# Ordering the first and last 128 columns so that their 64 KB stores have 32, not 4, steps in the outer dimension

## Chip, cores and metric

One core of a Trainium2 chip. The metric is the device time of one execution in microseconds, the median over several executions, all fast, that is, none is over 1.5% above the fastest of its kernel. The span in the profile is some 1.8 us shorter than that time. Where two kernels are compared by runs, they ran on the same chip in the same rounds; where that is not so, the text says it.

## The reference

A polynomial-sketch linear attention (4 batches, 4 heads, 1088 tokens, head size 32), whose output becomes `x` of 4352 rows by 128, is followed by a mixture of 4 experts that are all computed for all rows:

```python
x = attn_out.transpose(0, 2, 1, 3).reshape(B * S, H * D)      # 4352 x 128
p = domain_probs / (domain_probs.sum(-1, keepdims=True) + 1e-09)
for e in range(4):
    h = np.maximum(x @ w1[e], 0.0)                            # 128 -> 1024
    out += p[:, e:e + 1] * (h @ w2[e])                        # 1024 -> 128
```

## The kernel before

The attention leaves `x` transposed in `xT`, 128 features by 4352 columns. A batch has 34 tokens for each of 32 groups; column `32*c + j` of a batch is token `34*j + c`. The columns are worked off in 11 chunks. Nine of them go through a Strassen-like scheme; the first and the last, of 128 columns, are "plain": their second product has the 128 tokens on the partitions, so that the result can be stored as it is, without a transpose. With 128 columns a plain chunk holds four token offsets of each of the 32 groups, and partition `32*a + j` is token `34*j + c + a`.

```python
def keep_warm(n):                      # products on zeros: TensorE busy before its data are there
    for _ in range(n):
        wp = psum(ps_h, "h")
        nc.tensor.matmul(wp[:, :], warm[:, 0:P], warm[:, :], start=True, stop=True)
keep_warm(11)
...
for i, t in enumerate((0, (B - 1) * S + G - 4)):          # gate rows of the two plain chunks
    nc.sync.dma_start(
        ends[:, i, :], bass.AP(domain_probs.tensor, domain_probs.offset + t * E, [[E, 4], [G * E, 32], [1, E]]))
...
nc.vector.tensor_tensor(                                  # last product of the attention
    out=xT[:, S * b + c : S * b + c + n], in0=nd[1][:, 0:n], in1=rb[:, 0:n], op=ALU.mult)
...
if e == E - 1:                                            # plain chunk: all four experts added up
    t = (START[m] // S) * S + START[m] % S // 32
    nc.sync.dma_start(
        bass.AP(out.tensor, out.offset + t * DM, [[DM, 4], [G * DM, 32], [1, DM]]), total.pop(m)[:, :])
```

The last of these stores is the last thing that the kernel does. The kernel is divided below into three parts that add up to the span: the *start*, up to the first expert matmul (`h<-xT,w_sb`); the *body*, from there to the issue of the last store; and the *end*, from that issue to the last instruction.

Of the kernel before, what the change touches and what calls it, by code (L numbers as in the profile page):

```python
# [11 lines left out]
ALU = mybir.AluOpType  # L12
# [4 lines left out]
def _ap(t, p0: int, np_: int, off: int, free):  # L17

    p = list(t.ap)[0]
    return bass.AP(t.tensor, t.offset + p0 * p[0] + off, [[p[0], np_]] + [list(d) for d in free])  # L20
# [3 lines left out]
def kernel(  # L24
# [23 lines left out]
    nc = tc.nc  # L48

    P = 128  # L50
    HP = 64
    B, H, S, D = q.shape
    E, DM, F = w1.shape
    R = 8
    R2 = 2 * R
    G = S // 32
# [26 lines left out]
    def psum(pool, tag):  # L83
        return pool.tile([P, 512], F32, tag=tag, name=tag)
# [59 lines left out]
    ends = cpool.tile([P, 2, E], F32, name="ends")  # L144
    e_sum = cpool.tile([P, 2, 3], F32, name="e_sum")
    for i, t in enumerate((0, (B - 1) * S + G - 4)):
        nc.sync.dma_start(
            ends[:, i, :], bass.AP(domain_probs.tensor, domain_probs.offset + t * E, [[E, 4], [G * E, 32], [1, E]])
        )
    load_rows(q, 0, "qn", slice(P, S))  # L150
    for e in range(E):
# [20 lines left out]
    def keep_warm(n):  # L172

        for _ in range(n):
            wp = psum(ps_h, "h")
            nc.tensor.matmul(wp[:, :], warm[:, 0:P], warm[:, :], start=True, stop=True)  # L176

    keep_warm(11)


    turn = [0]
# [2 lines left out]
    def on_side(out, weights, moving, **flags):  # L184

        s = turn[0]
        turn[0] = 1 - s
        nc.tensor.matmul(out(s), weights(s), moving(s), **flags)  # L188
# [114 lines left out]
    xT = cpool.tile([P, B * S], F32, name="xT")  # L303
# [115 lines left out]
    def attend(b, c, n, qp):  # L419


        nd = [psum(ps_n, "den"), psum(ps_n, "num")]
        for i in range(2):
            for _ in range(2):
                on_side(
                    lambda s: nd[i][half[s], 0:n],
                    lambda s: kvzs[b][:, s, 1 - i, :],
                    lambda s: qp[s][:, 0:n],
                    start=True,
                    stop=True,  # L430
                )
        yield
        dT = apool.tile([P, QW], F32, tag="dT", name="dT")
        nc.vector.transpose(dT[:, 0:n], nd[0][:, 0:n])
        yield
        rc = apool.tile([P, QW // 32], F32, tag="rc", name="rc")
        nc.vector.tensor_scalar(
            out=rc[:, 0 : n // 32], in0=_ap(dT, 0, P, 0, [[32, n // 32]]), scalar1=1e-6, scalar2=1.0, op0=ALU.add, op1=ALU.mult
        )
        nc.vector.reciprocal(rc[:, 0 : n // 32], rc[:, 0 : n // 32])  # L440
        rb = apool.tile([P, QW], F32, tag="rb", name="rb")
        nc.vector.transpose(
            _ap(rb, 0, P, 0, [[32, n // 32], [1, 32]]), _ap(rc, 0, P, 0, [[1, n // 32], [0, 32]])
        )
        yield
        nc.vector.tensor_tensor(
            out=xT[:, S * b + c : S * b + c + n], in0=nd[1][:, 0:n], in1=rb[:, 0:n], op=ALU.mult
        )
        have[0] += n
        yield  # L450

    def queries(b, c, n):
        qT = query_turn(b, c, n)
        yield
        yield
        yield
        qc = psum(ps_f, "f")
        both(qc[:, 0:n], sq[:, :], qT[:, 0:n], start=True, stop=True)
        yield
        qf = apool.tile([P, QW], F32, tag="qf", name="qf")  # L460
        nc.vector.stream_shuffle(in_=qc[:, 0:n], out=qf[:, 0:n], mask=mask_lo)
        yield
        nc.vector.tensor_tensor(out=qf[:, 0:n], in0=qc[:, 0:n], in1=qf[:, 0:n], op=ALU.add)
        yield
        qb = apool.tile([P, QW], F32, tag="qb", name="qb")
        nc.vector.stream_shuffle(in_=qf[:, 0:n], out=qb[:, 0:n], mask=mask_b)
        yield
        qp = query_tiles()
        for x in range(2):
            qa = apool.tile([P, QW], F32, tag="qa", name="qa")  # L470
            nc.vector.stream_shuffle(in_=qf[:, 0:n], out=qa[:, 0:n], mask=mask_a[x])
            yield
            for p in range(2):
                query_product(qp, p, x, n, qa, qb)
                yield
        yield
        yield
        yield from attend(b, c, n, qp)
# [18 lines left out]
    def start():  # L497
# [36 lines left out]
        for x in range(2):  # L534
            for p in range(2):
                query_product(qp, p, x, n, fq[1 + x], qb)
        key_divide(b, kv)
        first = attend(b, 0, n, qp)
        next(first)
        keep_warm(4)  # L540
# [20 lines left out]
    hid, acc, total = {}, {}, {}  # L561
    NP = FB // 2

    def plain(m):
        return m in (0, NC - 1)
# [57 lines left out]
    def second(i):  # L623
        m, kq = steps[i]
        n, (e, f) = CHUNKS[m], divmod(kq, NP)
        hd = hid.pop(i)
        if plain(m):

            if f == 0:
                acc[m] = psum(ps_o, f"o{e % 2}")  # L630
            for j in range(2):
                for _ in range(2):
                    on_side(
                        lambda s: acc[m][half[s], 0:DM],
                        lambda s: hd[:, n * j + HP * s : n * j + HP * s + HP],
                        lambda s: w2_sb[:, e, 2 * f + j, :],
                        start=(f == j == 0),
                        stop=(f == NP - 1 and j == 1),
                    )
            if f == NP - 1:  # L640
                p_e = ends[:, 1 if m else 0, e : e + 1]
                if e == 0:
                    total[m] = mpool.tile([P, P], F32, tag="end", name="end")
                    nc.vector.tensor_scalar(
                        out=total[m][:, :], in0=acc[m][:, 0:DM], scalar1=p_e, scalar2=None, op0=ALU.mult
                    )
                else:
                    nc.vector.scalar_tensor_tensor(  # L648
                        out=total[m][:, :], in0=acc[m][:, 0:DM], scalar=p_e, in1=total[m][:, :], op0=ALU.mult, op1=ALU.add
                    )  # L650
                if e == E - 1:
                    t = (START[m] // S) * S + START[m] % S // 32
                    nc.sync.dma_start(
                        bass.AP(out.tensor, out.offset + t * DM, [[DM, 4], [G * DM, 32], [1, DM]]), total.pop(m)[:, :]
                    )
            return
        if f == 0:
            acc[m, e] = [psum(ps_o, "o0"), psum(ps_o, "o1")]
            begun[:] = [0, 0]
        w = n // 2  # L660
        blk = lambda a, j: w2_sb[:, e, 2 * f + j, HP * a : HP * a + HP]
        new = lambda a: w2s[:, e, f, a, :]
        place = lambda a: hd[:, w * a : w * a + w]

        todo = (
            [(blk(0, 0), place(0)), (new(3), place(3)), (blk(0, 1), place(2)), (new(1), place(6))],
            [(new(2), place(5)), (new(0), place(4)), (blk(1, 1), place(7)), (new(1), place(6))],
        )
        at = [0, 0]
        for _ in range(7):  # L670
            s = turn[0]
            p = at[s]
            at[s] += 1

            fresh = p >= begun[s]
            begun[s] = max(begun[s], p + 1)
            wt, mv = todo[s][p]
            on_side(
                lambda s: acc[m, e][p // 2][half[s], w * (p % 2) : w * (p % 2) + w],
                lambda s: wt,  # L680
                lambda s: mv,
                start=(fresh and p % 2 == 0),
                stop=(f == NP - 1),
                skip_group_check=True,
            )
# [81 lines left out]
    for i in range(len(steps) + LA):  # L767
        if i < len(steps):
            m, kq = steps[i]
# [29 lines left out]
        if i >= LA:  # L799
            second(i - LA)  # L800
            mm, kk = steps[i - LA]
            if kk % NP == NP - 1 and not plain(mm):
                ending = chain(ending, gather(mm, kk // NP))
            else:
                next(ending, None)
# [29 lines left out]
```

## Time and profile before

| | before |
|---|---|
| time, median of 4 runs | 496.27 us (496.11 to 496.53) |
| profiled run: time, span | 495.9, 494.1 us |
| start: first expert matmul at | 14.10 us |
| body: 14.10 to 490.55 | 476.45 us, PE busy 476.04 |
| end: 490.55 to 494.12 | 3.57 us |
| last store: issue, first packet after issue, data | 0.60, 1.23, 0.92 us |

"First packet" and "data" (from the first packet's start to the last one's end) come from the trace's records of single DMA packets.

### The profile page before, as it was taken

Reading aid. Unit: us, or ns where it says so; the run is one execution under the profiler, and the core shown is the slowest. Engines: PE = TensorE matmul, PEld = TensorE weight load, DVE = VectorE, ACT = ScalarE, POOL = GpSimd, SP = SyncE. Lnnn points to the kernel's source line nnn. Section 1 sums busy time; section 2 is a strip of 40 time slices with the busy share of each in tenths; the row PEclk is TensorE's granted clock in tenths of the full one; section 3 lists DMA queues with packets and bytes.
Section 4 is the critical chain, followed back from the end, with each engine's and each line's share of the span. In section 5 each row is a group of like instructions: output and inputs, shape, how many; then the busy total and the mean of one; then the engine's idle time right before and its main releaser. Section 6 shows DMA issues by size and latency. Waiting matters only on the chain.

```text
span 494.1 us, 11020 instructions
## 1 busy us (share of the span) xinstructions
PE 487.7 (99%) x4435; PEld 373.7 (76%) x4435; DVE 323.2 (65%) x751; ACT 244.2 (49%) x487; POOL 227.2 (46%) x260
## 2 busy tenths in 40 slices
PE   8999999999999999999999999999999999999996
PEld 5887877777777777777777777777777777778996
DVE  6759666777677576758566647468656657765642
ACT  3344464545454634545445554445445445566751
POOL 6051464435445354425455445335455446555570
PEclk9999999999999999999999999999999999999999
DMA  7981030021002320021002100021001100110000
GB/s 215 277 294 54 2 90 3 1 87 21 0 2 87 85 73 0 1 87 23 0 2 86 21 1 1 2 86 22 2 1 54 22 1 1 44 23 2 15 3 17
DMA packets 29618, 22.36 MB, mean 45 GB/s; under 512 B 19968, under 2 KB 26752, under 8 KB 29184
## 3 DMA queue, kind: packets, MB, share of 16 engines
q1 hardware_dynamic: 29552, 21.66, 15.2%
q8 instruction: 35, 0.57, 0.5%
q14 instruction: 15, 0.12, 0.1%
q10 hardware_dynamic: 16, 0.00, 0.0%
HBM read 19.35 MB, written 2.31 MB: 44 GB/s over the span
## 4 chain that ended last, share of the span: by engine, by line
PE 98%; DVE 1%; DMA 0%; POOL 0%; issue 0%; DVEq 0%
PE h L188 50%; PE o L188 40%; PE f L188 4%; PE den L188 2%; PE num L188 2%; DMA s_raw<-in_S_dram 0%; PE h L176 0%; POOL sr L241 0%; POOL sp L236 0%; DVE end L648 0%; DVE s_e L200 0%; DVE kvz L374 0%; DVE s_f L200 0%; DVE s_T L228 0%; DVE s_hl L227 0%
## 5 line engine op out<-in xcount | busy, mean ns | idle before, releaser
L584 DVE SCALAR_TENSOR_TENSOR hid<-h,hid 128x256 f32<-128x256 f32 (+6 forms) x432 | 203.7, 472 | 146.9 <-ACT hid L609 138.7
L188 PE MATMUL h<-xT,w_sb 128*64 128x512 f32 (+4 forms) x1408 | 298.3, 495 | 0.4 <-PE h L176 0.4
L609 ACT ACTIVATE hid<-h 128x512 f32<-128x512 f32 (+3 forms) x288 | 158.3, 550 | 200.3 <-PE h L188 167.1
L188 PE MATMUL o<-hid,w2s 128*64 128x256 f32 (+3 forms) x1152 | 222.0, 355 | 0.0
L188 PEld LDWEIGHTS h<-xT,w_sb 128*64 128x64 f32 x1408 | 151.2, 137 | 48.8 <-PE h L176 0.9
L188 PE MATMUL o<-hid,w_sb 128*64 128x256 f32 (+3 forms) x864 | 185.5, 355 | 0.0
L188 PEld LDWEIGHTS o<-hid,w2s 128*64 128x64 f32 x1152 | 131.7, 137 | 29.1
L724 POOL TENSOR_TENSOR ev<-yz,sh 64x256 f32<-64x256 f32 (+3 forms) x72 | 48.5, 673 | 159.7 <-ACT sh L727 157.0
L188 PEld LDWEIGHTS o<-hid,w_sb 128*64 128x64 f32 x864 | 102.0, 137 | 20.7
L712 POOL TENSOR_TENSOR yz<-ev 128x512 f32<-128x512 f32 (+3 forms) x36 | 41.9, 1164 | 69.0 <-ACT ev L715 68.8
L724 POOL TENSOR_TENSOR ct<-ev 128x512 f32<-128x512 f32 (+3 forms) x36 | 42.6, 1183 | 2.8
L724 POOL TENSOR_TENSOR ct<-ct,gate 128x512 f32<-128x512 f32 (+3 forms) x27 | 32.0, 1186 | 2.1
L724 POOL TENSOR_TENSOR total<-total,ct 128x512 f32<-128x512 f32 (+3 forms) x27 | 31.9, 1180 | 2.1
L412 DVE TENSOR_TENSOR qp<-qa,qb 64x352 f32<-64x352 f32 (+2 forms) x44 | 29.1, 661 | 1.1
L714 ACT COPY ev<-o 128x512 f32<-128x512 f32 (+3 forms) x36 | 19.3, 537 | 10.1 <-PE o L188 9.6
L188 PE MATMUL o<-w_sb,hid 128*64 128x128 f32 x256 | 22.4, 273 | 0.0
L715 ACT COPY ev<-o 128x512 f32<-128x512 f32 (+3 forms) x36 | 19.4, 538 | 2.5
L188 PEld LDWEIGHTS o<-w_sb,hid 128*64 128x64 f32 x256 | 19.0, 137 | 1.5 <-issue 0.2
L601 ACT ACTIVATE hid<-h 128x256 f32<-128x256 f32 x24 | 9.2, 383 | 21.4 <-PE h L188 20.9
L351 DVE TENSOR_TENSOR kp<-fs 128x256 f32<-128x256 f32 (+1 forms) x24 | 16.2, 682 | 0.0
L727 ACT COPY sh<-yz 64x256 f32<-64x256 f32 (+3 forms) x36 | 13.7, 379 | 1.6 <-POOL yz L712 0.8
L728 ACT COPY sh<-yz 64x256 f32<-64x256 f32 (+3 forms) x36 | 13.7, 379 | 0.9
(102 smaller groups left out, 244.0 us busy)
## 6 DMA issues: line engine op xcount, KB each, us to landing
w_sb<-in_moe_w_dram SPq DMA_DIRECT2D x8, 512.0 KB, 7.3
gate<-gates SPq DMA_DIRECT2D x3, 1024.0 KB, 4.4
kn<-in_k_dram SPq DMA_DIRECT2D x4, 544.0 KB, 4.4
vn<-in_v_dram SPq DMA_DIRECT2D x16, 128.0 KB, 4.1
gate<-gates SPq DMA_DIRECT2D x2, 960.0 KB
qn<-in_q_dram SPq DMA_DIRECT2D x3, 544.0 KB, 3.8
gate<-gates SPq DMA_DIRECT2D x1, 896.0 KB
out_dram<-ob SPq DMA_DIRECT2D x12, 64.0 KB, 2.0
```

Source lines behind the costliest of these rows:

```text
L188: nc.tensor.matmul(out(s), weights(s), moving(s), **flags)
L351: eng.tensor_tensor(out=_ap(kps[b], 0, P, 256 * t0 + P * p + 64 * x, [[256, n], [32, 2], [R, 4], [1, R]]), in0=_ap(src, 0, P, off + 4 * x, ...
L412: nc.vector.tensor_tensor(out=qp[p][64 * x : 64 * x + 64, 0:n], in0=qa[64 * p : 64 * p + 64, 0:n], in1=qb[64 * p : 64 * p + 64, 0:n], op=A ...
L584: nc.vector.scalar_tensor_tensor(out=out, in0=src, scalar=0.0, in1=in1, op0=ALU.max, op1=ALU.subtract)
L601: nc.scalar.activation(hd[:, 0 : 2 * n], hp[:, 0 : 2 * n], ACTF.Relu)
L609: nc.scalar.activation(hd[:, n * j : n * j + n], hp[:, 0:n], ACTF.Relu)
L712: add = lambda out, in0, in1, op=ALU.add: nc.gpsimd.tensor_tensor(out=out, in0=in0, in1=in1, op=op)
L714: nc.scalar.copy(_ap(ev, 0, P, 0, [[2 * w, 2], [1, w]]), _ap(a0, 0, P, 0, two))
L715: nc.scalar.copy(_ap(ev, 0, P, w, [[2 * w, 2], [1, w]]), _ap(a1, 0, P, 0, two))
L724: add = lambda out, in0, in1, op=ALU.add: nc.gpsimd.tensor_tensor(out=out, in0=in0, in1=in1, op=op)
L727: nc.scalar.copy(sh[HP:P, 0:w], yz[0:HP, 0, 0:w])
L728: nc.scalar.copy(sh[0:HP, 0:w], yz[HP:P, 1, 0:w])
```

## The change

Its intent is that the last store should run on all 16 DMA engines. The plain chunks' columns are put into `xT` in the order `4*j + a` instead of `32*a + j`, so that partition `4*j + a` is token `34*j + c + a`; in the output those are 32 steps of 4 rows that lie together. The gate rows are loaded in the same order. One of the warm-up products goes.

```diff
-            ends[:, i, :], bass.AP(..., [[E, 4], [G * E, 32], [1, E]])
+            ends[:, i, :], bass.AP(..., [[G * E, 32], [1, 4 * E]])
...
-    keep_warm(11)
+    keep_warm(10)
...
-        nc.vector.tensor_tensor(
-            out=xT[:, S * b + c : S * b + c + n], in0=nd[1][:, 0:n], in1=rb[:, 0:n], op=ALU.mult
-        )
+        end = B * S - P
+        turned = n if b == c == 0 else max(0, S * b + c + n - end)
+        if turned < n:
+            nc.vector.tensor_tensor(out=xT[:, S * b + c : S * b + c + n - turned],
+                in0=nd[1][:, 0 : n - turned], in1=rb[:, 0 : n - turned], op=ALU.mult)
+        if turned:
+            nc.vector.tensor_tensor(
+                out=_ap(xT, 0, P, end if b else 0, [[1, 4], [4, 32]]),
+                in0=nd[1][:, n - P : n].rearrange("p (g j) -> p g j", j=32),
+                in1=rb[:, n - P : n].rearrange("p (g j) -> p g j", j=32),
+                op=ALU.mult)
...
-                        bass.AP(out.tensor, out.offset + t * DM, [[DM, 4], [G * DM, 32], [1, DM]]), ...
+                        bass.AP(out.tensor, out.offset + t * DM, [[G * DM, 32], [1, 4 * DM]]), ...
```

More of the change, by code (lines that the diff above doesn't have):

```diff
@@ L147 @@
         nc.sync.dma_start(
-            ends[:, i, :], bass.AP(domain_probs.tensor, domain_probs.offset + t * E, [[E, 4], [G * E, 32], [1, E]])
+            ends[:, i, :], bass.AP(domain_probs.tensor, domain_probs.offset + t * E, [[G * E, 32], [1, 4 * E]])
         )
@@ L445, in attend @@
         yield
-        nc.vector.tensor_tensor(
-            out=xT[:, S * b + c : S * b + c + n], in0=nd[1][:, 0:n], in1=rb[:, 0:n], op=ALU.mult
-        )
+        end = B * S - P
+        turned = n if b == c == 0 else max(0, S * b + c + n - end)
+        if turned < n:
+            nc.vector.tensor_tensor(
+                out=xT[:, S * b + c : S * b + c + n - turned], in0=nd[1][:, 0 : n - turned], in1=rb[:, 0 : n - turned], op=ALU.mult
+            )
+        if turned:
+            nc.vector.tensor_tensor(
+                out=_ap(xT, 0, P, end if b else 0, [[1, 4], [4, 32]]),
+                in0=nd[1][:, n - P : n].rearrange("p (g j) -> p g j", j=32),
+                in1=rb[:, n - P : n].rearrange("p (g j) -> p g j", j=32),
+                op=ALU.mult,
+            )
         have[0] += n
@@ L653, in second @@
                     nc.sync.dma_start(
-                        bass.AP(out.tensor, out.offset + t * DM, [[DM, 4], [G * DM, 32], [1, DM]]), total.pop(m)[:, :]
+                        bass.AP(out.tensor, out.offset + t * DM, [[G * DM, 32], [1, 4 * DM]]), total.pop(m)[:, :]
                     )
```

## The prediction

> **What bounds the kernel now.** I read the page's busy table and chain first, then each engine's busy time in three stretches (start, body, end), then the end in order of time.
>
> ```profile
> PE 487.7 (99%) x4435; PEld 373.7 (76%) x4435; DVE 323.2 (65%) x751; ACT 244.2 (49%) x487; POOL 227.2 (46%) x260
> ...
> PE 98%; DVE 1%; DMA 0%; POOL 0%; issue 0%; DVEq 0%
> ```
>
> The TensorE is busy for 99% of the span and carries 98% of the chain of work that ended last. The stretches say where the other few microseconds are (columns: length, then busy time of PE, PEld, DVE, ACT, POOL, then granted clock, DMA share, GB/s):
>
> ```profile
> 14.10:30.00 15.90, 15.90 (x248) 14.64 (x250) 11.51 (x29) 6.13 (x16) 3.27 (x6) 1.00 0.90 292
> 30.00:480.00 450.00, 450.00 (x3818) 341.30 (x3816) 298.30 (x671) 231.58 (x453) 213.73 (x217) 1.00 0.11 32
> ...
> 490.55:494.10 3.55, 0.00 (x0) 0.00 (x0) 0.00 (x0) 0.00 (x0) 0.00 (x0) 0.84 0.07 18
> ```
>
> From 14.1 to about 490 us PE never rests, so in that stretch only a change of PE's own work can move the time, and this change touches none of it. What is open is the start, before 14.1, and the last 3.55 us, in which no compute engine works. The timeline of the end, and the waits of the DMA queue there, tell what those 3.55 us are:
>
> ```profile
> 488.62 1.52 PE L188 MATMUL o<-w_sb,hid 128*64 128x128 f32 x23
> 490.18 0.35 DVE L648 SCALAR_TENSOR_TENSOR end<-o,ends,end 128x128 f32<-128x128 f32 x1 [0.89 <-PE o L188]
> 490.55 0.60 SPq L653 DMA_DIRECT2D out_dram<-end  x1
> ```
>
> ```profile
> SPq L830 <- DMA out_dram<-end: 1.9, 1, 1.9
> SPq L830 <- PEq L830: 0.6, 2, 0.4
> ```
>
> The last product ends, VectorE adds the last expert, the SP queue issues one 64 KB store for 0.60 us, then waits 1.9 us for it. So the store takes 0.60 + 1.9 = 2.5 us from issue to release, wholly on the path, and about 1.0 us of closing barrier follows (490.55 + 2.5 = 493.05; the span is 494.1).
>
> The DMA view of the stretch 490.5 to 493.0, whose 40 slices are 0.0625 us each, shows how it moves:
>
> ```profile
> GB/s 0 0 0 0 0 0 0 0 0 0 0 0 0 0 0 0 0 0 0 0 16 49 33 49 49 90 98 74 90 98 74 90 98 74 66 0 0 0 0 0
> DMA packets 132, 0.07 MB, mean 26 GB/s; under 512 B 4, under 2 KB 132, under 8 KB 132
> ```
>
> Twenty idle slices, then fifteen with data: the first packet is at 491.75, 1.2 us after issue; the data run for 15 x 0.0625 = 0.94 us; release comes 0.36 us after them. 128 packets carry 512 B each; four small ones are left over.
>
> [...]
>
> [...] The new product writes fp32 with a step of 4 elements, 16 bytes[...]. No row of the trace before has such a write[...].
>
> [...] the first warm-up products start 0.43 us apart (1.19, then 1.59, 2.02), and near 4.9 us the spacing falls.
>
> **The change part by part.**
>
> *Last store, removed time.* 128 packets over 4 engines are 32 each, and the data took 0.94 us, or 29 ns a packet. Over 16 engines they are 8 each: 8 x 29 = 0.24 us, so 0.70 less. The issue should shrink as well. A 16-engine store of the same kind just before (32 KB, issued at 484.94) had an issue of 0.32 us and its first packet 0.81 us after issue, against 0.60 and 1.2 here; I count 0.3. Together 2.5 - 0.70 - 0.3 = 1.5. A second estimate, from DMA rows that ran on 16 engines:
>
> ```profile
> out_dram<-ob SPq DMA_DIRECT2D x12, 64.0 KB, 2.0
> ...
> out_dram<-ob SPq DMA_DIRECT2D x4, 8.0 KB, 1.5
> out_dram<-ob SPq DMA_DIRECT2D x4, 16.0 KB, 1.5
> ```
>
> These move 128-byte packets: 512, 64 and 128 of them. The new store has 128 packets, like the 16 KB one (1.5 us), each four times as long: about 1.6 us. I take 1.55, so the store gives 2.5 - 1.55 = 0.95 us. Nothing lies beside it; the whole of it leaves the span.
>
> *First store* (issued at 36.4): the same saving, but PE is busy there and no later load is waited for. 0.
>
> *Loads of the gate rows.* The two `ends` loads go from 4 to 16 engines; their issues (1.29 us together) may fall by some 0.5 us, so the weights behind them start earlier. The first weight block is issued at 7.26 and lands 6.0 us later, at 13.3; its first use is at 14.06. The next is issued at 7.73, lands 7.3 later at 15.0, and is used at 16.2. They wait for nobody, so earlier is worth 0.
>
> *One warm-up product fewer.* The relevant lines of the start:
>
> ```profile
> 1.19 4.34 PE L176 MATMUL h<-warm 128*128 128x512 bf16 x11 [1.19 <-DVE s_hl L212]
> 5.84 2.32 PE L188 MATMUL h<-sk,kT 128*64 128x64 f32 x72 [0.31 <-POOL sr L241]
> ...
> 13.70 0.29 DVE L446 TENSOR_TENSOR xT<-num,rb 128x128 f32<-128x128 f32 x1
> 14.10 1.53 PE L188 MATMUL h<-xT,w_sb 128*64 128x128 f32 x24 [0.44 <-PE h L176]
> ```
>
> Warm-ups end at 5.53 and PE then waits 0.31 us for GpSimd. With ten they end near 5.3 and the wait is 0.5; the next work still starts at 5.84.[...] 0.
>
> *Reordered product.* The first `xT` product (13.70, 0.29 us) is on the path to the first expert matmul at 14.10, which shows as a wait for PE's warm-up but really follows this write. Same elements, one instruction for one. If every element cost a second cycle, 128 elements at the slope of these products ((652 - 292) ns over (480 - 128) columns = 1.0 ns an element) would cost 0.13 us more. I count half, 0.06. The last unit's product splits into 224 and 128 columns at 439.6 us: one more start of some 0.16 us (292 - 128 x 1.0) on VectorE, plus at most the same 0.13. VectorE has idle gaps before its next rectify steps, and the matmul that reads them runs two steps later. 0. The built instruction lists agree: VectorE gains that one instruction, PE loses one load and one product at the start, and every other engine keeps its order and count.
>
> Sum: -0.95 + 0.06 = -0.89 us, so 496.31 - 0.89 = 495.42.
>
> **The rivals.** *Fixed latency rules the store.* If most of the 2.5 us is start and receipt, and sixteen completions come no sooner than four, only the data time shrinks, perhaps by 0.4: 495.9. Against it, the 16-engine stores land in 1.5 us with as many packets. *The strided write or the first microseconds cost more*, either because the write is slower than I allow[...]: if the 72 products from 5.84 on began at half rate this costs up to 1 us and eats the gain, 496.3.[...] *Loads gain*: were a weight wait hidden at 14.06 or 16.2 (PEld shows two gaps of 0.2 there), 0.2 to 0.4 us more would come out, 495.0. Landing times speak against it.
>
> **Range and chances.** All of these stay within about 1 us, 0.2% of the whole; 2% would be 9.9 us, more than the whole idle end. Runs before spread over 0.3 us. I predict 495.4 us, 8 in 10 between 494.9 and 496.1; faster by over 2% 0.01, within 2% 0.98, slower 0.01.
>
> **What would show it.** Sixteen small packets beside the 128 in the last store; its data in some 0.3 us; issue near 0.4 us; the final wait about 1.1 us instead of 1.9; the end 2.6 to 2.8 us after its issue. The first expert matmul within 0.1 us of 14.10, and PE unbroken after it. Wrong would be: a store on 16 engines that lands no sooner than 2.0 us, a first expert matmul later than 14.3, or a body (14.1 to the last issue) longer or shorter by more than 0.3 us.

The four engines of the old store are in the trace of before: while its data moved (491.80 to 492.70) the busy share of the 16 DMA engines was 0.26, as much as 4.2 busy engines. The sixteen of the `ob` stores are there too: the four stores from 484.94 have 64 small packets. That the new store would have sixteen was assumed; the result below shows it. The 0.06 for the reordered product was an estimate from the slope of the other products, 1.0 ns an element, as the trace of before has no such write. The second rival's "half rate" is the spacing of the first warm-ups, 0.43 us, against 0.22 between the last two; what makes it fall is not shown there (the granted clock reads 1.00 in every stretch up to 14.1).

## The result

The changed kernel takes 495.75 us (median of 4 runs, 495.43 to 496.28) against 496.27 (496.11 to 496.53). The ratio, which is the mean time of one kernel's fast runs over that of the other's of the same rounds and so not quite the ratio of the medians, is 0.999, with a 95% interval of 0.9973 to 1.0007. Five more runs of the same kernel gave 495.69 against 496.28 (0.9976 to 1.0001). Both intervals reach 1, so the times alone do not show a gain; what shows it is the end of the profiles below, which repeats. The medians put it at 0.5 to 0.6 us of some 496, in the direction foretold and about 60% of the 0.89 foretold.

The end of the changed kernel in order of time, and the waits of its DMA queue there:

```profile
490.24 0.35 DVE L659 SCALAR_TENSOR_TENSOR end<-o,ends,end 128x128 f32<-128x128 f32 x1 [0.89 <-PE o L188]
490.62 0.58 SPq L664 DMA_DIRECT2D out_dram<-end  x1
```

```profile
SPq L841 <- DMA out_dram<-end: 1.4, 1, 1.4
SPq L841 <- PEq L841: 0.6, 2, 0.4
```

The wait fell from 1.9 to 1.4 us. The issue did not get shorter: 0.58 against 0.60. The DMA view of the same stretch as in the prediction (490.5 to 493.0, slices of 0.0625 us) says the rest:

```profile
GB/s 0 0 0 0 0 0 0 0 0 0 0 0 0 0 0 0 0 0 0 0 0 41 172 303 279 189 66 0 0 0 0 0 0 0 0 0 0 0 0 0
DMA packets 144, 0.07 MB, mean 26 GB/s; under 512 B 16, under 2 KB 144, under 8 KB 144
```

There are sixteen small packets where there were four, and in both traces each is followed 0.32 to 0.35 us later by one semaphore update, so they are called completion packets below. In 491.95 to 492.05 the busy share of the 16 DMA engines is 1.04, as much as sixteen busy engines (0.26 before, over its data). The whole trace has 48 packets under 512 B more than that of before (20016 against 19968), which is 12 for each of the four transfers that changed, two stores and two gate loads. There are six slices with data where there were fifteen. But the data begin in slice 21 (slice 20 before, with the issue 0.07 us earlier), just as late as before: by the packets' records 1.24 us after the issue (before 1.23). Only the data time shrank, from 0.92 to 0.36 us.

The body is unchanged. In the table by stretches each row has the length, then the busy time and instructions of PE, PEld, DVE, ACT and POOL; the first row is the kernel before, the second the changed one:

```profile
14.10:490.55 476.45, 476.04 (x4244) 365.84 (x4244) 314.21 (x711) 239.63 (x474) 219.24 (x225) 1.00 0.14 40
```

```profile
14.16:490.62 476.46, 476.04 (x4244) 366.05 (x4244) 314.23 (x712) 239.64 (x474) 219.22 (x225) 1.00 0.14 40
```

The start got 0.06 us longer (14.10 to 14.16), although its key products began 0.03 earlier (5.81 against 5.84). The new product shows why: 0.39 us instead of 0.29, and the first expert matmul now waits for it openly.

```profile
5.81 2.32 PE L188 MATMUL h<-sk,kT 128*64 128x64 f32 x72 [0.54 <-DVE kT L312]
...
13.68 0.39 DVE L454 TENSOR_TENSOR xT<-num,rb 128x128 f32<-128x128 f32 x1
14.16 1.53 PE L188 MATMUL h<-xT,w_sb 128*64 128x128 f32 x24 [0.53 <-DVE xT L454]
```

The sum of the profiled runs: start +0.06, body +0.01, end 3.57 to 3.03, that is -0.54; together -0.47, and the spans are 494.12 and 493.65.

### The profile page after: what moved, and what is told of

Its sections match the earlier page's. It is cut to its first block, busy times and chain, and to the rows that moved or that the text cites. A ratio compares the mean times of both kernels' runs of the same rounds, so it can differ in the third digit from the quotient of the medians.

```text
span 493.7 us, 11019 instructions
## 1 busy us (share of the span) xinstructions
PE 487.5 (99%) x4434; PEld 373.8 (76%) x4434; DVE 323.3 (65%) x752; ACT 244.2 (49%) x487; POOL 227.1 (46%) x260
## 2 busy tenths in 40 slices
DMA packets 29666, 22.36 MB, mean 45 GB/s; under 512 B 20016, under 2 KB 26800, under 8 KB 29232
## 4 chain that ended last, share of the span: by engine, by line
PE 98%; DMA 1%; DVE 0%; issue 0%; SPq 0%; DVEq 0%
PE h L188 50%; PE o L188 40%; PE f L188 4%; PE den L188 2%; PE num L188 2%; DMA kn<-in_k_dram 1%; PE h L176 0%; DVE kT L312 0%; SPq L119 0%; DVE xT L454 0%; DVE end L659 0%; DVE kvz L374 0%; DVEq L374 0%
```

## The experiments

Twelve runs followed, one of them the changed kernel again. Several give a wrong result: they store rows in the wrong places, or reorder columns and not rows. Their engines do the same work, so their times count (but for store_rows3, which stores half of the bytes). This table has the profiles of all of them except store_rows3 in the three parts; the median is beside that of the kernel before in the same rounds. The single runs of store_k8, store_k2 and store_rows3 are not known to be fast, and only their profiles are used. All times in us.

| kernel | first expert matmul | last store issued | issue | first packet | data | span | median (runs), before |
|---|---|---|---|---|---|---|---|
| before | 14.10 | 490.55 | 0.60 | 1.23 | 0.92 | 494.12 | 496.27 (4) |
| changed | 14.16 | 490.62 | 0.58 | 1.24 | 0.36 | 493.65 | 495.75 (4), 496.27 |
| store_only | 14.25 | 490.71 | 0.59 | 1.24 | 0.36 | 493.73 | 495.67 (5), 496.28 |
| turn_only | 14.39 | 490.85 | 0.60 | 1.24 | 0.92 | 494.42 | 496.24 (5), 496.28 |
| after_warm11 | 14.86 | 491.32 | 0.58 | 1.24 | 0.36 | 494.33 | 495.77 (5), 496.28 |
| after_again | 14.68 | 491.24 | 0.58 | 1.24 | 0.35 | 494.24 | 495.69 (5), 496.28 |
| store_rows | 14.14 | 490.60 | 0.35 | 0.85 | 0.36 | 493.22 | 495.17 (5), 496.22 |
| store_k8 | 14.13 | 490.59 | 0.66 | 1.29 | 0.58 | 493.86 | 495.64 (1), 496.22 |
| store_k2 | 14.66 | 491.11 | 0.57 | 1.21 | 1.76 | 495.48 | 497.26 (1), 496.22 |
| last_only | 14.04 | 490.54 | 0.62 | 1.27 | 0.35 | 493.59 | 495.48 (5), 496.22 |
| last_two | 14.13 | 490.58 | 0.62, ACT 0.66 | 1.26 | 0.53 | 493.80 | 495.59 (5), 496.21 |
| four_stores | 14.13 | 490.59 | 0.79 for two | 0.82 | 0.78 | 493.66 | 495.51 (5), 496.21 |
| after_warm14 | 14.66 | 491.12 | 0.58 | 1.24 | 0.36 | 494.14 | 495.81 (5), 496.21 |

The distance from the first expert matmul to the last issue is 476.45 to 476.50 in all rows except after_again, where it is 476.56. So a difference between two spans is a difference of the start or of the end, and the two can be read apart. The start varies from run to run of one kernel by some 0.5 us, which is as large as the effect; the end does not: from the last issue to the end of the span it is 3.00 to 3.05 us in the six profiles with the new store alone at the end, and 3.57 in both with the old one.

**Theory A:** the gain is the data time of the last store alone, and the new product takes part of it back. **Rival B:** the issue shrinks with 16 engines too. **Rival C:** the start differs for other reasons than the product.

### store_only: the new stores without the rest

```diff
-    [[DM, 4], [G * DM, 32], [1, DM]]
+    [[G * DM, 32], [1, 4 * DM]]
```

> The kernel before with one edit: the two 128-row stores go to 32 groups of 4 rows. Wrong on purpose: rows of the first and last 128 end up permuted. Theory A (the gain is the store's data time alone: 32 packets of 512 B on each of 4 engines become 8 on each of 16): issue stays at 0.60 us, first packet 1.2 us after issue, data 0.36 us instead of 0.93, the last wait 1.3 to 1.4 us instead of 1.9, first expert matmul as before (14.1 give or take 0.05); time 0.5 to 0.6 us below before, a little better than the full change. Rival B (the issue shrinks too with 16 engines, and only the profile after was an unlucky one): issue near 0.4, first packet 0.8 to 0.9 after issue, wait near 1.1, time 0.9 below.

Measured: issue 0.59, first packet 1.24, data 0.36, wait 1.4; 495.67 against 496.28. Theory A holds and B falls: with 16 engines alone the issue stays.

```profile
490.71 0.59 SPq L653 DMA_DIRECT2D out_dram<-end  x1
SPq L830 <- DMA out_dram<-end: 1.4, 1, 1.4
```

The first expert matmul is at 14.25, later than foretold, and for a reason that has nothing to do with the store: the key load came later (key products at 6.00). The product is 0.29 us, and the matmul follows it 0.39 us after its start, as before.

### turn_only: the reordered product without the rest

```diff
-    out=xT[...: ... + n], in0=nd[1][:, 0:n], in1=rb[:, 0:n]
+    (the product in one or two parts, as in the change; old stores, loads and warm-ups)
```

> The kernel before with only the reordered xT product, and the old stores, loads and 11 warm-up products. Wrong on purpose: the first and last 128 rows are permuted. Theory A (the 16-byte-step write costs 0.10 us on the path of the start, and the split at the end of the attention costs nothing): first xT product 0.39 us instead of 0.29, its two-part form at 439.6 us unseen by PE, time 0.05 to 0.15 us above before. Rival C (the write costs nothing and the 0.1 of the first expert matmul came from loads landing later in that one run): product 0.29, time as before.

Measured: the product takes 0.38 us, and the first expert matmul starts 0.48 us after its start (13.91 and 14.39), against 0.40 before (13.70 and 14.10). So the write with a step of 16 bytes costs 0.08 to 0.09 us on the path.

```profile
13.91 0.38 DVE L454 TENSOR_TENSOR xT<-num,rb 128x128 f32<-128x128 f32 x1
14.39 1.53 PE L188 MATMUL h<-xT,w_sb 128*64 128x128 f32 x24 [0.53 <-PE h L176]
```

In four profiles the four-by-32 products take 383 to 394 ns, against 292: 0.09 to 0.10 us for 128 elements. Whether the step itself costs this, or the pattern of two levels in which the new product is written, no run separates. Rival C falls as an explanation of the product, but the total does not resolve so small a cost: 496.24 against 496.28. That its two-part form at the end of the attention costs nothing shows in the body, which is the same in all kernels.

### after_warm11, after_again and after_warm14: the warm-up products

```diff
-    keep_warm(10)
+    keep_warm(11)        # after_warm14: keep_warm(14); after_again: the changed kernel as it is
```

> The changed kernel with the eleventh warm-up product put back. Correct result. If the warm-up count is neutral (mine): PE idle 0.3 instead of 0.5 us before the first key products, those products 2.32 us for 72 as before and after, time equal to the changed kernel within 0.2 us. Rival:[...] this version is faster than the changed kernel by 0.3 us or more, and does not show its spread of 0.85 us.

> The changed kernel unchanged, on the same chip and in the same rounds as the other three, to have its time against them. Store theory: 0.4 to 0.5 us below before (0.5 to 0.6 from the store, less 0.1 of the first product). If the fixed part of the start varies (key load or projection load landing last), the spread of 0.8 us seen before is seen in all four kernels and in the kernel before as well.

> The changed kernel with 14 warm-up products instead of 10. Correct result. At 0.427 us each[...] 14 products last from 1.19 to 7.2[...], against 5.6 for ten and the 5.8 to 6.0 at which the keys are there. Theory: the warm-ups become the bound of the start[...], so the time rises by 0.2 to 1.2 us, unevenly from run to run. Rival (warm-ups are free): time as the changed kernel.

After_warm11 and after_again took 495.77 and 495.69: no difference. But their profiles show that my reason for it does not hold in every run. These are the warm-ups and the first key products of turn_only (11 warm-ups) and of after_again (10):

```profile
1.19 4.88 PE L176 MATMUL h<-warm 128*128 128x512 bf16 x11 [1.19 <-DVE s_hl L212]
6.00 2.33 PE L188 MATMUL h<-sk,kT 128*64 128x64 f32 x72
```

```profile
1.19 4.45 PE L176 MATMUL h<-warm 128*128 128x512 bf16 x10 [1.19 <-DVE s_hl L212]
6.07 2.57 PE L188 MATMUL h<-sk,kT 128*64 128x64 f32 x72 [0.43 <-DVE kT L312]
```

In the kernel before, eleven took 4.34 us, because near the end the spacing of their starts fell from 0.43 to 0.22 us. In turn_only they took 4.88, and in after_warm11 4.87, near to eleven times 0.43: the spacing fell later, there was no wait left before the key products, and in after_warm11 those took 2.80 us instead of 2.32. In after_again all ten were slow (4.45) and so were the first key products (2.57). So the moment at which the spacing falls differs between executions of one kernel; it fell 3.0 us after the first warm-up in store_only, and had not fallen 4.2 us after it in turn_only. The cause is not shown: the granted clock in the records is 1.00 over the first 14.1 us of all these profiles. After_again's start is 0.52 us longer than that of the same kernel in the first profile (14.68 against 14.16); of these, the key load gives 0.26 (6.07 against 5.81) and the slow key products 0.25. This is the spread of the times, and after_warm11 has it too (495.42 to 496.12), as does the kernel before (496.03 to 496.68 in nine runs).

The trace of before puts the wait for the key products down to GpSimd. But in ten of the fourteen profiles, before among them, they start 0.86 us after the first transpose of the keys (`kT`), whenever the key load lets that start (4.93 to 5.22), so it is the keys that they follow. In turn_only, after_warm11 and store_k2 they start 0.94, 0.99 and 0.98 us after it, straight behind the eleventh warm-up: where the spacing falls late and the keys come early, the eleventh costs 0.08 to 0.13 us (in store_rows3 the keys came as late as it, and it cost nothing). That this is what the removed product was for is only argued.

With 14 the wait is there even though the spacing falls on the way (they took 5.16 us, against 14 times 0.43, or 6.0): in after_warm14's profile the key products start at 6.29, 1.28 us after the transpose, or 0.42 later than the keys allow. Its median, 495.81, is still 0.4 below that of before and only some 0.1 above the changed kernel's in other rounds; the runs do not resolve such a cost. It was less than I expected.

### store_rows, store_k8, store_k2: engines and the form of the store

Theory A leaves a question open: why do other stores on 16 engines have a shorter issue and an earlier first packet? **Theory D:** because of their form, not of their engines. A store whose two sides have the same outer count is issued sooner than one in which the 128 partitions must be matched with 32 groups of 4. **Rival E:** any store of 128 partitions takes 0.6 us.

```diff
-    [[DM, 4], [G * DM, 32], [1, DM]]
+    [[DM, 128], [1, DM]]                 # store_rows: 128 rows that lie together
+    [[DM, 8], [8 * DM, 16], [1, DM]]     # store_k8
+    [[DM, 2], [2 * DM, 64], [1, DM]]     # store_k2
```

> The kernel before with the two 128-row stores written to 128 rows that lie together (so one row per partition, 128 in the outer dimension on both sides, two dimensions). Wrong on purpose. Theory D (the issue of 0.60 us and the first packet 1.2 us after it belong to the form in which the 128 partitions must be cut into groups to match the destination; the stores and loads whose two sides have the same outer count issue in 0.32 to 0.46): issue near 0.4, first packet 0.8 to 1.0 after issue, data 0.36, so the last wait 1.3 or less counted from a shorter issue; time 0.7 to 0.9 below before. Rival E (0.6 us is what any store of 128 partitions takes): issue 0.58 to 0.60, first packet 1.2, everything as in the run with only the new store, time 0.5 to 0.6 below before.

> As above with 8 in the outer dimension (8 x 16 rows of 512 B). Wrong on purpose. Engine theory: 8 small completion packets, 16 data packets per engine, data 16 x 23 ns plus some 0.15 us of staggered start = 0.5 us, between the 0.92 of four engines and the 0.36 of sixteen; issue 0.6. Rival (the long data time of before came from 512 B runs in the destination rather than 2 KB runs): 0.9 us of data here too, since the runs are the same 512 B steps.

> As above with 2 in the outer dimension (2 x 64 rows). Wrong on purpose. Engine theory: 2 completion packets, 64 data packets per engine, data 64 x 23 ns plus 0.15 = 1.6 us, issue still 0.6, last wait 0.7 us longer than before, near 2.6, time 0.7 above before. Rival as above: data 0.9 as before.

The end of store_rows, then its DMA view of 490.5 to 493.0:

```profile
490.22 0.35 DVE L648 SCALAR_TENSOR_TENSOR end<-o,ends,end 128x128 f32<-128x128 f32 x1 [0.89 <-PE o L188]
490.60 0.35 SPq L653 DMA_DIRECT2D out_dram<-end  x1
```

```profile
GB/s 0 0 0 0 0 0 0 0 0 0 0 0 0 0 0 123 262 311 222 115 17 0 0 0 0 0 0 0 0 0 0 0 0 0 0 0 0 0 0 0
DMA packets 144, 0.07 MB, mean 26 GB/s; under 512 B 16, under 2 KB 144, under 8 KB 144
```

Theory D fits, and E falls. With the same 128 packets on the same 16 engines, the issue is 0.35 instead of 0.58, the data begin in slice 15 instead of 21 (0.85 us after the issue instead of 1.24), and take the same 0.36. The last wait is 1.2 us, and the DMA view gives 1.6 us from issue to landing, against 2.0 for the changed kernel. The time is 495.17 against 496.22, ratio 0.9983 (0.9970 to 0.9997): 1.05 us below by the medians, 0.84 by the ratio, and its end is 0.95 shorter in the profile. The 0.4 us between its end (2.62) and that of store_only (3.02) is the price of the form. The first store of the kernel, in the middle of other work, agrees: its issue is 0.36 in store_rows and 0.60 to 0.68 in the thirteen other profiles. One more property differs: the 128 rows of store_rows leave no gaps in the output. Four_stores below has equal counts, 32 on both sides, and gaps, and its first packet still comes after 0.82, so gaps alone are not the cause.

Store_k8 and store_k2 have 8 and 2 small packets, and their data take 0.58 and 1.76 us. With 2, 4, 8 and 16 engines (the busy share of the 16 in the DMA views is one tenth in store_k2 and at most five tenths in store_k8) the data take 1.76, 0.92, 0.58 and 0.36. At the 27 ns that most of these packets last, 64, 32, 16 and 8 packets in a row make 1.73, 0.86, 0.43 and 0.22; the rest, 0.03 to 0.15, fits engines that do not run in step: in the changed kernel the sixteen completion packets lie up to 0.15 us apart. (The 23 ns of the expectations fit the difference of 0.56 us between 32 and 8 packets in a row.) So the engines explain the data time, also where the destination's runs are 512 B as before; the rival, which would have the runs explain it, falls. (Store_k2's one time, 1.0 above before, holds 0.5 from a slow start.) Their issues are 0.66 and 0.57 and their first packets 1.29 and 1.21 after: the issue does not follow the number of engines.

### store_rows3: an attempt to separate the form from the number of dimensions

```diff
+    bass.AP(out.tensor, out.offset + t * DM, [[DM, P], [64, 2], [1, 32]]), _ap(total, 0, P, 0, [[32, 2], [1, 32]])
```

> The kernel before with its two 128-row stores written as 128 rows that lie together, each in two runs of 128 B with a gap (three dimensions, 128 in the outer one on both sides, half of the bytes, 256 packets of 128 B). Wrong on purpose. If what costs time in the issue is that the 128 partitions have to be cut to match the destination: issue 0.35 to 0.4, first packet 0.8 to 0.9 after it, in spite of three dimensions. Rival (three dimensions cost it): issue 0.57 to 0.66 and first packet 1.2 to 1.3, as in the other stores with three.

The issue was 0.58 us, the first packet came 1.23 after it, and the wait was 1.3; one run took 496.01 us, with a slow start (14.77). But the build had merged the destination into 256 runs, so that its outer count was 256 against the source's 128: unequal counts again. The run agrees with theory D, and separates nothing: a store with three dimensions and equal counts on 128 partitions was not tried. What the traces do have are loads of that kind. In the trace of before, the second weight block of each expert (line 127) has three dimensions with 128 in the outer one on both sides, and three of the four issue in 0.43 us (the fourth took 0.65, among loads whose issue was held up for as much as 3.78); a load of 128 rows of 512 B with gaps between them (`qn`) issues in 0.42:

```profile
L127 SPq DMA_DIRECT2D w_sb<-in_moe_w_dram x4: 433/434/649, 7.7 to 16.4; - x4
1.62 0.42 SPq L93 DMA_DIRECT2D qn<-in_q_dram  x1
```

The stores of `ob` (three dimensions, 32 on both sides) issue in 0.32 to 0.46 there. So neither three dimensions nor gaps raise an issue to 0.6 us in these traces; for a store of 128 partitions that is argued from the loads, not shown.

### last_only, last_two, four_stores: can both kernels be beaten?

```diff
-    turned = n if b == c == 0 else max(0, S * b + c + n - end)
+    turned = max(0, S * b + c + n - end)      # last_only; first chunk, its gate rows and its store as before

+    for s, eng in enumerate((nc.sync, nc.scalar)):   # last_two: last_only, store in halves of 64 partitions
+        eng.dma_start(bass.AP(out.tensor, out.offset + (t + 16 * G * s) * DM, [[G * DM, 16], [1, 4 * DM]]), tot[half[s], :])

+    for g in range(4):                               # four_stores: old order, ten warm-ups, 32 partitions each
+        (nc.sync, nc.scalar)[g % 2].dma_start(
+            bass.AP(out.tensor, out.offset + (t + g) * DM, [[G * DM, 32], [1, DM]]), tot[32 * g : 32 * g + 32, :])
```

> The changed kernel with only the last chunk reordered; the first chunk's product, gate rows and store stay as before. Correct result. Theory: the 0.10 us of the 16-byte-step write leaves the path of the start (product 0.29 us), the end is that of the changed kernel (wait 1.4), so 0.1 us below the changed kernel, 0.5 to 0.7 below before. Rival (the first store on 4 engines or the start cost elsewhere): no better than the changed kernel, 0.5 below before.

> The version with only the last chunk reordered, its store cut into two of 64 partitions (16 rows of 4 tokens each), one on the SP queue, one on ACT's. Correct result. If the issue time grows with the packets that the cut form has to make (64 instead of 128): issues of some 0.45 us side by side, first packets about 1.05 us after issue, last wait shorter by 0.15, time 0.1 to 0.2 below the version with one store. If the cut form costs a fixed 0.6: nothing gained, or 0.1 lost to ACT's slower issue.

> The kernel before (old column order, ten warm-up products), with only the last store cut into four of 32 partitions, one for each token offset, so that the outer count of both sides is 32 without any cut of the partitions; two on the SP queue, two on ACT's. Correct result. Theory D: issue 0.32 to 0.45 each, the second pair issued 0.4 after the first, its first packet 0.84 after that, 32 packets on 16 engines in 0.15: last data 1.4 us after the first issue, against 1.59 for the changed kernel and 2.15 before; time 0.7 to 0.8 below before, 0.1 to 0.2 below the changed kernel. Rival: four stores on two queues get in each other's way, or ACT's issue is slow (0.58 for its one load at the start), and the end is that of the changed kernel or later.

Last_only does what was expected: its first product is 0.29 us again, its start 14.04, its end that of the changed kernel, and its time 495.48 against 496.22 (ratio 0.9986, 0.9973 to 0.9998). It has the lowest median of the correct kernels here, though its gain over before exceeds that of the changed kernel by only 0.15 to 0.22 us, in other rounds, which is less than the runs resolve. Last_two gained nothing: the issues stay 0.62 and 0.66 with half the packets, so the cost of the form did not fall with the number of packets, and the data of the two halves follow one another. Four_stores needs no reordering at all. Its issues are short (0.33 to 0.42 each) and its first packet comes 0.82 us after, but the second pair waits for the first:

```profile
490.59 0.79 SPq L656 DMA_DIRECT2D out_dram<-end  x2
490.59 0.84 ACTq L656 DMA_DIRECT2D out_dram<-end  x2
```

The last data end 1.59 us after the first issue, as in the changed kernel, so for the end of the profile the rival was right. Its time is 495.51 against 496.21 (ratio 0.9987, 0.9974 to 0.9999); that gain of 0.70 is what theory D foretold, but not for its reason: the end is no shorter (3.07 us against 3.03), while the first product keeps its 0.29 us.

## Why the prediction was right or wrong

*The time, its range and the class* were right: 495.75 against 495.4, between 494.9 and 496.1. The range owes this in part to its width: it holds every gain from 0.2 to 1.4 us, the rival's 0.4 too. The gain was too large by 0.3 to 0.4 us, and the failing is in one term.

*Last store, 0.95 us.* Measured 0.54 at the end of the profiled run, 0.55 in store_only. The term has two parts. The data time was right in kind and nearly in size: 0.92 to 0.36 is 0.57 less, where 0.70 was foretold: eight packets in a row were counted, and the sixteen engines finish up to 0.15 us apart. The step that failed is "The issue should shrink as well": 0.3 us were counted for issue and first packet, and it was 0.0 (issue 0.60 to 0.58, first packet 1.23 to 1.24). The number came from a store that differed from this one in engines and in form (32 partitions, equal counts), and I gave the difference to the engines. It was also the shortest of four alike: the three issued straight behind it took 0.45 to 0.46. The second estimate, 1.55 from the rows of `ob`, failed for the same reason and so confirmed nothing: all of those rows have the form with equal outer counts. Store_rows, which has that form, lands in just the foretold 1.6. By the prediction's own signs this step is the wrong one: it named as wrong a store on 16 engines that lands no sooner than 2.0 us, and the changed store lands in 2.0; the issue was to be near 0.4 (0.58), the last wait 1.1 (1.4), and the end 2.6 to 2.8 (3.03).

*First store* 0: right; the body is the same. *Gate loads* 0: right in worth, wrong in the step. Their two issues took 1.30 us against 1.29, not 0.5 less; they too have 128 partitions against 32 groups, on whichever number of engines.

*One warm-up fewer,* 0: right for the time, within what runs resolve. The reason given was that the products had become faster before the eleventh; the spacing shows that in some profiles (0.22 us before the eleventh in before), but in turn_only and after_warm11 the eleventh was the last to finish. Nor did the key products wait for GpSimd there; they follow the keys.

*Reordered product,* 0.06: measured 0.08 to 0.09 on the path. The product became longer by 0.09 to 0.10 us, about three quarters of the 0.13 taken as its most; whether the step of 16 bytes or the pattern of two levels is the reason, no run separates. *Its split at 439.6 us,* 0: right, PE rests nowhere in the body.

*The rivals.* "Fixed latency rules the store" put the time at 495.9 and its gain at 0.4; the measured gain lies between this and the prediction, and in kind this rival was right. "More at the start" names the place of the spread, the moment at which the products become faster (eleven warm-ups took 4.01 to 4.88 us), but it strikes both kernels: the sign "a first expert matmul later than 14.3" came in after_again (14.68), and with eleven warm-ups and the old order in store_k2 (14.66) too. "Loads gain" did not happen.

## What to carry to other kernels

A store that ends a kernel has three parts that can be read from packet records: from issue to first packet, data, and release (1.23, 0.92 and 0.33 us in before); ask of each which property of the transfer moves it. The number of engines moved only the data part here (0.92 to 0.36 us), while equal outer counts on both sides moved the first part by 0.4 us: issue 0.35 and first packet after 0.85 us with 128 on both sides, 0.57 to 0.66 and 1.21 to 1.29 where the counts differ, on 2 to 16 engines alike and with 64 to 256 packets. Counted from the end of the issue, the first packet came after 0.49 and 0.50 us where the counts are equal (four_stores, store_rows) and 0.63 to 0.66 where they are not. When a duration is borrowed from another transfer, compare all of its properties, not only the one that the change is about; and divide the span into start, body and end before a difference of half a microsecond is explained, since the start alone varied by as much between executions of one kernel.
